# Output staging, a merged addition and interleaved token rows in a local and strided attention with an FFN

## The chip, the cores and the metric

One core of one Trainium2 chip runs the whole program. The metric is the device time of one execution in microseconds (us); times are medians over runs. TensorE multiplies matrices and writes PSUM; VectorE (DVE), ScalarE (ACT) and GpSimd (POOL) do elementwise work; SyncE (SP) issues all the DMA transfers. Each engine works through its own queue in a fixed order, and an instruction that waits holds up all that is behind it.

## The reference

Inputs q, k, v have the shape (8 batch entries, 8 heads, 576 tokens, 64). Heads 0 to 3 see a local window, heads 4 to 7 every 32nd token. The attention's output, 4608 tokens by 512, goes through a two-layer network with GELU between.

```python
pos = np.arange(S)
rel = pos[:, None] - pos[None, :]
mask_local = (rel >= 0) & (rel < 32)
mask_strided = (rel >= 0) & (pos[None, :] % 32 == pos[:, None] % 32)
scores = np.where(masks, scale * (q @ k.T), -1e9)
x = (softmax(scores) @ v).transpose(0, 2, 1, 3).reshape(4608, 512)
h = x @ w_in                      # 512 x 2048
g = 0.5 * h * (1 + erf(h / sqrt(2)))
out = g @ w_out                   # 2048 x 512
```

## The kernel before, in words

**Tiles.** The 4608 tokens are cut into rows of 32, 16 rows (512 tokens) make a tile, and there are nine tiles, t = 0 to 8. `order_of_rows` (line 110) says which rows: after the first two tiles, all of a batch entry's rows 4 to 17 follow one another, and the last tile holds rows 16 and 17 of entry 6 and rows 4 to 17 of entry 7. The hidden 2048 columns are 16 slices f of 128. Every operand of a matmul is split into a high and a low part, and a product is the sum of three matmuls (high by high, low by high, high by low).

**Plain tiles (0 to 2, `ffn`).** For each f: the product with w_in into a PSUM bank H0 or H1 (line 991), GELU and a copy of the high part on ACT (L1017, L1018), the low part on DVE (L1020), and four output blocks a = 0 to 3 of 128 tokens, accumulated over f in the banks O0 to O3 (`second`, L1041).

**Crossed tiles (3 to 8, `crossed`, `pair`).** The first product is made in the manner of Strassen and Winograd: two slices f = 2p and 2p + 1 form a cycle p, with seven block products instead of eight, each of six matmuls of 256 columns (`product`, L1190). The weights of a block product are loaded from HBM into one of 22 pieces of memory in turn (L1179); two of these lie in the buffer `xll`. Half of the token columns are even rows, half are odd rows, so in these tiles the rows of the output stand in the order 0, 2, 4, ..., 14, 1, 3, ..., 15 of the tile. A cycle has two banks; the products 1, 6 and 7 accumulate in one half of the second, and copies of it (L1218, ACT or DVE) and of product 5 go to the memory `extra`. DVE additions (`plus`, L1224) put them together: `c11` after product 2, `c12` after product 3, both 256 columns in the two halves of the first bank, and `c22` after product 7, which product 4 then accumulates on. GELU (L1250), the copy of the high part (L1251) and the low part (L1253) follow for each of the two banks. The GELU results rotate through three pairs of buffers (`third`).

**Order.** TensorE's order is written by hand: a string of products and output blocks of the cycle before, `"1oo256o37oo4ooo"`, where o is one output block (the first four are those of slice 2p, the next those of 2p + 1). All other engines' orders come from a planner (`Plan.run`): a list scheduler with a cost and a due time for each operation. From 140 us of planned time on (`steady`) it holds back work on ACT and DVE that would delay operations marked urgent, such as these copies, additions and GELUs. It counts 0.05 us from the end of an operation to its user (0.2 for TensorE) and 0.6 us on SP for the storing of a block.

**Storing (`leave`).** After the last f, each output block is copied from its bank by ACT or DVE (L1069) into a staging buffer and stored (L1088). From tile 2 on there are two staging buffers in `xlh`: blocks 0 and 2 share one, 1 and 3 the other, and the copy waits for the store before. In crossed tiles a block's four rows of 32 tokens aren't neighbours in the output, so it leaves in four transfers of 64 KB. In the last tile block 3 is made in two halves of 256 columns: its last two slices accumulate in two spare banks, and DVE adds them to what was copied early to another buffer (L1067, L1280).

**Strided heads.** Their attention is done without TensorE: POOL multiplies (L885, L902), DVE sums up (L890, L907), with batch entries' data loaded at L869. The local heads use TensorE (L589, L634) and DVE and ACT for the softmax (L652, L659).

## Time and profile before

| what | value |
|---|---|
| median of 3 runs | 845.63 us (845.23 to 846.0) |
| the profiled execution | 843.62 us |
| its span, first to last instruction | 841.8 us |
| mean granted clock of TensorE | 0.997 |
| TensorE busy | 810.8 us, 96% |
| DVE, ACT, POOL busy | 576.5, 475.7, 522.7 us |
| DMA moved | 172.62 MB |

The span is what the trace covers; 1.82 us of the execution lie outside it. A busy engine isn't a bound by itself; the chain of waits tells which work the end of the program hung on, and the timeline of an engine shows in brackets how long it sat idle before an instruction and what ended that.

### The profile page before, as it was taken

The numbers are of one execution on the slowest core, as the hardware profiler recorded it, in microseconds if no ns is written. First come the engines' busy times: TensorE is split into PE (matmuls) and PEld (weight loads), VectorE is DVE, ScalarE is ACT, GpSimd is POOL, SyncE is SP. The second block draws the span as 40 slices with busy tenths as digits, with TensorE's granted clock in tenths as the row PEclk, the third lists the DMA queues.
The fourth block names the chain that finished last, engine by engine and source line by source line (L and its number), as shares of the span: only waits on it lengthen the run. The fifth ranks groups of instructions, "written<-read, shape, count | busy, mean of one in ns | idle before, by whom it ended". The sixth has DMA issues, their size and how long they took to land.

```text
span 841.8 us, 18074 instructions
## 1 busy us (share of the span) xinstructions
PE 810.8 (96%) x6702; PEld 707.7 (84%) x6702; DVE 576.5 (68%) x1248; ACT 475.7 (57%) x1006; POOL 522.7 (62%) x448
## 2 busy tenths in 40 slices
PE   2899999999999999999999999999999999999996
PEld 2788888888888888989898989898889889898995
DVE  6887866866666778677877786577876787353332
ACT  6799955753584368546654676455745573232221
POOL 5736678799878877895777677646985576000000
PEclk9999999999999999999999999999999999999998
DMA  9947467323635677667876776768677576466401
GB/s 351 425 190 288 139 183 255 124 71 124 194 132 165 226 230 249 223 216 236 254 228 208 236 263 182 260 209 245 218 248 252 179 250 199 146 194 207 151 1 50
DMA packets 85430, 172.62 MB, mean 205 GB/s; under 512 B 10336, under 2 KB 24928, under 8 KB 83040
## 3 DMA queue, kind: packets, MB, share of 16 engines
q1 hardware_dynamic: 85344, 171.48, 61.1%
q8 instruction: 53, 0.87, 0.4%
q14 instruction: 33, 0.27, 0.1%
HBM read 143.13 MB, written 24.12 MB: 199 GB/s over the span
## 4 chain that ended last, share of the span: by engine, by line
PE 91%; DVE 2%; ACT 2%; DMA 2%; issue 1%; SPq 1%; POOL 0%; DVEq 0%; ACTq 0%; POOLq 0%
PE banks L1041 45%; PE banks L1190 27%; PE banks L991 15%; PE banks L634 2%; PE banks L589 1%; DMA sv<-in_vs_dram 1%; DMA out_dram<-xlh_ob 1%; DMA lq_qk<-in_qk_dram 1%; PE banks L608 1%; SPq L1088 0%; DVE xsl L777 0%; DVE banks L1224 0%; SPq L1179 0%; ACT w_pt L659 0%; DVE pt L652 0%
## 5 line engine op out<-in xcount | busy, mean ns | idle before, releaser
L1190 PE MATMUL banks<-w_wt,w_wt 128*128 128x256 f32 x1308 | 186.5, 284 | 2.3 <-DVE gl_all L1253 1.7
L1190 PEld LDWEIGHTS banks<-w_wt,w_wt 128*128 128x128 f32 x1308 | 173.6, 191 | 10.2 <-DVE gl_all L1253 1.9
L1041 PE MATMUL banks<-w_wt,gh_all 128*128 128x512 f32 (+1 forms) x514 | 160.6, 394 | 0.0
L1250 ACT ACTIVATE banks<-banks 128x512 f32<-128x512 f32 x96 | 55.9, 582 | 130.8 <-DVE banks L1224 95.3
L1041 PE MATMUL banks<-w_wt,gh 128*128 128x512 f32 x384 | 118.4, 389 | 0.0
L1224 DVE TENSOR_TENSOR banks<-banks,w_extra 128x256 f32<-128x256 f32 x144 | 61.2, 428 | 80.5 <-PE banks L1190 71.4
L1041 PE MATMUL banks<-w_wt,gl_all 128*128 128x512 f32 (+1 forms) x257 | 99.8, 388 | 0.0
L1041 PEld LDWEIGHTS banks<-w_wt,gh_all 128*128 128x128 f32 x514 | 88.5, 190 | 11.3
L1041 PE MATMUL banks<-w_wt,w_wt 128*128 128x512 f32 x360 | 95.4, 393 | 0.0
L1041 PEld LDWEIGHTS banks<-w_wt,gh 128*128 128x128 f32 x384 | 71.7, 188 | 14.5
L1041 PE MATMUL banks<-w_wt,gl 128*128 128x512 f32 x192 | 74.8, 390 | 1.0 <-DVE gl L1020 1.0
L1041 PEld LDWEIGHTS banks<-w_wt,w_wt 128*128 128x128 f32 x360 | 63.7, 189 | 10.1
L1218 ACT COPY w_extra<-banks 128x256 f32<-128x256 f32 x69 | 24.3, 374 | 84.0 <-DVE banks L1224 42.6
L1190 PEld LDWEIGHTS banks<-xsh,w_wt 128*128 128x128 f32 x352 | 53.3, 188 | 12.4 <-ACT w_extra L1218 3.5
L1020 DVE TENSOR_TENSOR gl<-banks,gh 128x512 fp32r<-128x512 f32 (+1 forms) x50 | 33.4, 667 | 41.9 <-ACT gh L1018 41.8
L1253 DVE TENSOR_TENSOR gl_all<-banks,gh_all 128x512 fp32r<-128x512 f32 x64 | 44.0, 687 | 25.2 <-ACT gh_all L1251 24.5
L1017 ACT ACTIVATE banks<-banks 128x512 f32<-128x512 f32 (+1 forms) x50 | 28.4, 567 | 56.7 <-PE banks L991 56.5
L1190 PE MATMUL banks<-xsh,w_wt 128*128 128x256 f32 x352 | 56.7, 283 | 2.7 <-ACT w_extra L1218 1.9
L1041 PEld LDWEIGHTS banks<-w_wt,gl_all 128*128 128x128 f32 x257 | 48.3, 188 | 10.8
L991 PE MATMUL banks<-xsh,w_wt 128*128 128x512 f32 (+1 forms) x200 | 54.2, 389 | 0.0
L991 PE MATMUL banks<-xlh,w_wt 128*128 128x512 f32 (+1 forms) x200 | 53.2, 384 | 0.0
L1218 DVE COPY w_extra<-banks 128x256 f32<-128x256 f32 x75 | 30.5, 420 | 19.3 <-PE banks L1190 18.2
(893 smaller groups left out, 1809.0 us busy)
## 6 DMA issues: line engine op xcount, KB each, us to landing
w_wt<-block SPq DMA_DIRECT2D x306, 256.0 KB, 3.1
w_raw<-in_w_dram SPq DMA_DIRECT2D x16, 1023.8 KB, 12.4
lq_qk<-in_qk_dram SPq DMA_DIRECT2D x8, 1280.0 KB, 5.8
lq_v<-in_vl_dram SPq DMA_DIRECT2D x8, 1024.0 KB, 5.4
block<-w_extra SPq DMA_DIRECT2D x32, 256.0 KB, 2.6
xll_all<-block SPq DMA_DIRECT2D x30, 256.0 KB, 2.9
block<-w_wt SPq DMA_DIRECT2D x24, 256.0 KB, 3.5
out_dram<-xlh_ob SPq DMA_DIRECT2D x92, 64.0 KB, 2.2
```

Of the source, the lines that this page charges most:

```text
L589: nc.tensor.matmul(sb[j][i]()[quarter(g), c + r * 64:c + (r + 1) * 64], qv[half(i), r, a, b * QB:(b + 1) * QB], kv[half(i), r, a, b * QB:( ...
L608: nc.tensor.matmul(x, vv[quarter(g), c, h, :], pv[quarter(g), c, h, :], start=(c == 0), stop=(c == g % 2), tile_position=(g * QB, i * 64))
L634: nc.tensor.matmul(xb[b]()[half(i), c:c + QB], vv[half(b), a, 2 * r + i, :], bv[half(b), a, 2 * r + i, :], start=True, stop=True, tile_pos ...
L991: nc.tensor.matmul(hp()[:, 0:c1 - c0], w1[f][:, lw, c, :], rx, start=((c, part) == (2, 0)), stop=((c, part) == end))
L1017: A.activation(hp()[:, 0:N], hp()[:, 0:N], AF.Gelu)
L1020: o3 = plan.add({"DVE": dve(N)}, lambda e, hp=hp, a_=a_, b_=b_, N=N: V.tensor_tensor(b_()[:, 0:N], hp()[:, 0:N], a_()[:, 0:N].bitcast(F32) ...
L1041: nc.tensor.matmul(acc()[:, 0:d1 - d0], x().bitcast(F32R)[:, c:c + P], w2[f][:, y, d0:d1], start=start and i == 0, stop=stop and i == 2)
L1190: nc.tensor.matmul(acc(), w[:, a, c, :], x[b][:, c, :], start=first and n == 0, stop=n == 5, skip_group_check=not first)
L1218: o = plan.add({"ACT": act(256), "DVE": dve(256)}, lambda e: (V.tensor_copy if e == "DVE" else A.copy)(dst(), src()), deps + old, 0, src.b ...
L1224: o = plan.add({"DVE": dve(256)}, lambda e: V.tensor_tensor(dst(), a(), b(), ALU.add), deps, 0, a.banks + dst.banks + [extra], name=name)
L1250: A.activation(hb(), hb(), AF.Gelu)
L1253: d = plan.add({"DVE": dve(TT)}, lambda e, hb=hb, gh=gh, gl=gl: V.tensor_tensor(gl().bitcast(F32R), hb(), gh().bitcast(F32), ALU.subtract) ...
```

## The change

Staging: `xll` becomes staging too, so that from tile 2 on each of the four blocks has a buffer of its own (blocks 0 and 1 in `xlh`, 2 and 3 in `xll`); the ring of weight pieces goes from 22 to 20. Addition: `c11` and `c12` become one DVE addition of 512 columns after product 3. Last tile: the copy of the high part and the low part of the GELU are written with the 32 tokens of a block's four rows interleaved (token m of row c at place 4m + c of the block), so that a block whose rows lie evenly in one batch entry leaves in one transfer; its blocks are finished in the order 0, 2, 1, 3, with blocks 0 and 1 copied by ACT and 2 and 3 by DVE. TensorE's order in the first crossed cycle becomes `"1o256o37o4o"` (it has four output blocks to place). The three GELU buffer pairs are used in another order. The planner counts 0.5 us after a POOL operation and 5% more for its duration, from 140 us on.

```diff
+ORDERS = "1o256o37o4o", "1oo256o37oo4ooo"
+    POOL_LAT = 0.5
...
-            at[op] = max([d.end + (self.PE_LAT if d.engine == "PE" else self.LAT) for d in op.deps] + [op.rel])
+            at[op] = max([d.end + (self.PE_LAT if d.engine == "PE" else self.POOL_LAT if d.engine == "POOL" and d.end > self.steady
+                                   else self.LAT) for d in op.deps] + [op.rel])
...
-                dur = op.eng[e]
+                dur = op.eng[e] * (1.05 if e == "POOL" and now > self.steady else 1.0)
...
-        for a in range(NJ):
-            k = a % 2, t < PLAIN - 1
+        for a in (0, 2, 1, 3) if last else range(NJ):
+            k = (a if t >= PLAIN - 1 else a % 2), t < PLAIN - 1
...
-                ob, first = Area(staged[0], a % 2 * DM, DM), free.get(NF - 1)
+                ob, first = Area(staged[a // 2], a % 2 * DM, DM), free.get(NF - 1)
...
-                    "DVE" if a % 2 else "ACT": 0.7 / n}
+                    "DVE" if a > 1 else "ACT": 0.7 / n}
...
+                    by = 1 if t < PLAIN else 2
                     runs = []
                     for i, (b, r) in enumerate(rows):
-                        if runs and rows[i - 1] == (b, r - 1):
+                        if runs and rows[i - 1] == (b, r - by):
...
+                    if last and len(runs) == 1:
+                        to = out[runs[0][2]:runs[0][2] + QB, cols]
+                        to = bass.AP(tensor=to.tensor, offset=to.offset, ap=[
+                            [DM, QB], [by * QB * DM, 4], [1, cols.stop - cols.start]])
+                        nc.sync.dma_start(to, ob()[:, cols])
+                        return
                     for c0, c1, d in runs:
-                        nc.sync.dma_start(out[d:d + (c1 - c0) * QB, cols], ob()[c0 * QB:c1 * QB, cols])
+                        if by == 1:
+                            nc.sync.dma_start(out[d:d + (c1 - c0) * QB, cols], ob()[c0 * QB:c1 * QB, cols])
+                            continue
+                        for c in range(c0, c1):
+                            e = d + (c - c0) * by * QB
+                            nc.sync.dma_start(out[e:e + QB, cols], ob()[c:P:4, cols] if last else ob()[c * QB:(c + 1) * QB, cols])
...
-        staged.append(buf("xlh", [P, N2, TT], "ob", 1, F32, mats))
-        xl = buf("xll", [P, N2, TT], "all", 1, F32R, mats)
+        staged.extend([buf("xlh", [P, N2, TT], "ob", 1, F32, mats), buf("xll", [P, N2, TT], "ob", 1, F32, mats)])
...
-        pieces.extend([(Area(xl, x * DM, DM), [h_last[NF - 1]], xl) for x in range(2)])
+        third.append([Area(held[NF - 1], 2 * DM * x, DM) for x in range(2)])
         third.extend([buf(x, [P, TT], f"all{i}", 2, F32R, mats) for x in ("gh", "gl")] for i in range(2))
-        third.append([Area(held[NF - 1], 2 * DM * x, DM) for x in range(2)])
...
+    def by_rows(x, t):
+        return x().rearrange("p (a c m) -> p a c m", a=NJ, m=QB) if t == NT - 1 else x()
+
+    def turned_rows(x, t):
+        return x().rearrange("p (a m c) -> p a c m", a=NJ, m=QB) if t == NT - 1 else x()
...
-        c11 = plus(r1, r1, s1, [P_[2], k1], f"c{t}.{p}.11")
...
-        c12 = plus(r3, r3, s2, [P_[3], k2], f"c{t}.{p}.12")
+        c1 = plan.add({"DVE": dve(512)}, lambda e: V.tensor_tensor(bi(), bi(), Area(extra, 1024, 512)(), ALU.add),
+                      [P_[2], P_[3], k1, k2], 0, [bi, extra], name=f"c{t}.{p}.1")
+        c1.urgent = URGENT[1]
...
-                A.copy(gh().bitcast(F32R), hb())
+                A.copy(turned_rows(gh, t).bitcast(F32R), by_rows(hb, t))
...
-                gl().bitcast(F32R), hb(), gh().bitcast(F32), ALU.subtract), [g], 0, [hb] + hold, name=f"gl{t}.{f}")
+                turned_rows(gl, t).bitcast(F32R), by_rows(hb, t), turned_rows(gh, t).bitcast(F32), ALU.subtract), [g], 0, [hb] + hold, name=f"gl{t}.{f}")
...
-        for x in "1oo256o37oo4ooo":
+        for x in ORDERS[c is not cycles[0]]:
...
-    for x, y in zip(*cycles[-1]["o"]):
-        plan.pe += [x, y]
+    x, y = cycles[-1]["o"]
+    for a in (0, 2, 1, 3, 4):
+        plan.pe += [x[a], y[a]]
```

## Rows read from the trace of the kernel before

**Rows 1.** The page's chain of waits, shares of the span by engine.
```profile
PE 91%; DVE 2%; ACT 2%; DMA 2%; issue 1%; SPq 1%; POOL 0%; DVEq 0%; ACTq 0%; POOLq 0%
```
**Rows 2.** Busy time by stretches: stretch, length, then PE, PEld, DVE, ACT, POOL, clock, DMA.
```profile
40.00:298.00 258.00, 258.00 (x1856) 213.29 (x1855) 183.98 (x350) 166.13 (x315) 196.66 (x161) 1.00 0.51 176
363.30:826.40 463.10, 460.28 (x3917) 412.70 (x3917) 310.55 (x690) 234.04 (x517) 247.59 (x204) 1.00 0.64 206
```
**Rows 3.** Timeline of PE: start, duration, line, operation; in brackets idle before, releaser.
```profile
307.95 0.98 PE L1190 MATMUL banks<-w_wt,w_wt 128*128 128x256 f32 x6 [1.73 <-DVE gl_all L1253]
...
360.30 0.97 PE L1190 MATMUL banks<-w_wt,w_wt 128*128 128x256 f32 x6 [0.48 <-DVE banks L1224]
...
402.42 0.73 PE L1190 MATMUL banks<-xsh,w_wt 128*128 128x256 f32 x4 [0.31 <-DVE w_extra L1218]
...
446.68 0.74 PE L1190 MATMUL banks<-xsh,w_wt 128*128 128x256 f32 x4 [0.19 <-ACT w_extra L1218]
...
492.00 0.74 PE L1190 MATMUL banks<-xsh,w_wt 128*128 128x256 f32 x4 [0.67 <-ACT w_extra L1218]
...
593.68 0.73 PE L1190 MATMUL banks<-xsh,w_wt 128*128 128x256 f32 x4 [1.06 <-ACT w_extra L1218]
...
759.34 0.74 PE L1190 MATMUL banks<-xsh,w_wt 128*128 128x256 f32 x4 [0.52 <-DVE w_extra L1218]
```
**Rows 4.** Timeline of the end, from 828 us on.
```profile
830.49 3.62 SPq L1088 DMA_DIRECT2D out_dram<-xlh_ob  x8
...
834.03 0.42 DVE L1067 TENSOR_TENSOR lead_all<-banks,lead_all 128x256 f32<-128x256 f32 x1 [0.22 <-PE banks L1041]
834.21 1.77 SPq L1088 DMA_DIRECT2D out_dram<-lead_all  x4
...
837.95 1.77 SPq L1088 DMA_DIRECT2D out_dram<-lead_all  x4
```
**Rows 5.** Timeline of SP at the end of tile 2: stores of whole blocks.
```profile
300.23 1.03 SPq L1088 DMA_DIRECT2D out_dram<-xlh_ob  x2
```
**Rows 6.** DMA issues: count, KB each, median us from issue to landing.
```profile
out_dram<-xlh_ob SPq DMA_DIRECT2D x3, 256.0 KB, 2.6
...
out_dram<-lead_all SPq DMA_DIRECT2D x8, 32.0 KB, 1.6
```
**Rows 7.** Timeline, block copies that waited for a store.
```profile
491.08 0.58 ACT L1069 COPY xlh_ob<-banks 128x512 f32<-128x512 f32 x1 [1.91 <-DMA out_dram<-xlh_ob]
...
757.80 0.69 DVE L1069 COPY xlh_ob<-banks 128x512 f32<-128x512 f32 x1 [2.75 <-DMA out_dram<-xlh_ob]
```
**Rows 8.** Groups by line and shape: busy us, mean ns; idle before, releasers.
```profile
L1224 DVE TENSOR_TENSOR banks<-banks,w_extra 128x256 f32<-128x256 f32 x144 | 61.2, 428 | 80.5 <-PE banks L1190 71.4 <-issue 6.1 <-ACT pt L659 2.2
...
L1253 DVE TENSOR_TENSOR gl_all<-banks,gh_all 128x512 fp32r<-128x512 f32 x64 | 44.0, 687 | 25.2 <-ACT gh_all L1251 24.5
...
L496 ACT ACTIVATE w_raw<-lead_all 128x1024 int32<-128x1024 int16 x16 | 18.2, 1140 | 0.1
```
**Rows 9.** Timeline of a quiet cycle of the last tile, DVE and PE.
```profile
749.03 0.43 DVE L1224 TENSOR_TENSOR banks<-banks,w_extra 128x256 f32<-128x256 f32 x1 [0.90 <-PE banks L1190]
749.75 0.43 DVE L1224 TENSOR_TENSOR banks<-banks,w_extra 128x256 f32<-128x256 f32 x1 [0.29 <-PE banks L1190]
750.73 0.69 DVE L1253 TENSOR_TENSOR w_wt<-banks,w_wt 128x512 fp32r<-128x512 f32 x1 [0.55 <-ACT w_wt L1251]
...
753.71 0.88 PE L1190 MATMUL banks<-w_wt,w_wt 128*128 128x256 f32 x6
```
**Rows 10.** The chain in order of time: start, duration; one run of output blocks.
```profile
463.22 2.07 PE banks L1041 x9
```
**Rows 11.** Timeline of the first crossed cycle.
```profile
304.34 0.42 DVE L1224 TENSOR_TENSOR banks<-banks,w_extra 128x256 f32<-128x256 f32 x1
...
304.68 1.28 ACT L1250 ACT_TABLE_LOAD   x1
```
**Rows 12.** Timeline of DVE in tile 6: a sum waiting for POOL's product.
```profile
586.66 0.95 DVE L907 TENSOR_REDUCE acc_7.2_6609<-prod_v7.2.3_6588 128x64 f32<-128x768 f32 x1 [3.05 <-POOL prod_v7.2.3_6588 L902]
```

More of the change, by code (lines that the diff above doesn't have):

```diff
@@ L1242, in pair @@
         os_ = []
-        for f, hb, deps in ((i, bi, [c11, c12]), (j, bj, [P_[4], c22])):
+        for f, hb, deps in ((i, bi, [c1]), (j, bj, [P_[4], c22])):
             k = 2 * c + f - i
@@ L1266, in pair @@
             os_.append(row)
-        cycles.append({"p": P_, "o": os_, "adds": [c11, c12, c22], "t": t, "n": p})
+        cycles.append({"p": P_, "o": os_, "adds": [c1, c22], "t": t, "n": p})
     spare = [bank("S0"), bank("S1")]
```

## Prediction

> **What bounds the kernel now.** I read the chain of waits first, by engine [rows 1]: nine tenths of it is TensorE, and DVE, ACT and DMA have 2% each. So a cheaper DVE or ACT instruction is worth nothing by itself. Only three things can pay: time before TensorE starts, holes in its stream, and time after its last matmul. Next the busy time by stretches [rows 2]: from 40 to 298 us TensorE is busy for all of 258.00 us, and from 363.3 to 826.4 it lacks 463.10 - 460.28 = 2.82 us. The first 40 us stay as they are: the planner's new terms act from its 140th us on, and all other edits lie later. That leaves the holes and the end.
>
> Then the holes, from the timeline of TensorE alone [rows 3]: after 40 us there are seven, 1.73 + 0.48 + 0.31 + 0.19 + 0.67 + 1.06 + 0.52 = 4.96 us. Last the end [rows 4]: the last matmuls are taken by a DVE addition that ends at 834.03 + 0.42 = 834.45, and the span ends at 841.8. The 7.35 us between are SyncE issuing twelve more stores at 0.44 us each, and the last landing. Together 12.3 us (1.5% of the span) can be reached at all.
>
> **The end.** Before, blocks 0, 1 and 2 leave in four transfers each and block 3 in two halves of four: 20 issues, which keep SyncE occupied from 830.49 to 837.95 + 1.77 = 839.72, and the span ends 2.08 us later [rows 4]. With the new row order blocks 1 and 3 have rows of one batch entry (entry 7, rows 10, 12, 14, 16 and 11, 13, 15, 17), so block 1 takes one issue and each half of block 3 one. Blocks 0 and 2 begin with row 16 or 17 of entry 6, so they have two runs and still leave in four: 4 + 4 + 1 + 1 + 1 = 11 issues, the quick blocks last. Block 0 keeps its start, and block 2 takes the place of block 1, so the first eight end at 830.49 + 3.62 = 834.11, as now. An issue of 256 KB in one piece took 1.03 / 2 = 0.52 us [rows 5]; with 0.1 us before each (834.11 to 834.21 [rows 4]) three make 1.86 and end at 836.0. The data of block 3, ready at 834.45, no longer comes last. The landing: 32 KB took 1.6 us and 256 KB 2.6 [rows 6], the new last piece has 128 KB, so I add 0.5: 836.0 + 2.08 + 0.5 = 838.6, **3.2 us earlier**. Bounds: with issues of 0.44 and no longer landing it ends at 834.11 + 3 x 0.44 + 2.08 = 837.5 (4.3 gained); with issues of 0.88 (twice that, for a pattern of three levels) and a landing 1.0 longer, 834.11 + 2.64 + 3.08 = 839.8 (2.0 gained). I stay near the middle, by the 256 KB row, the same kind of store.
>
> **Four staging buffers.** Now two blocks share one buffer, so the copy of the third block waits until the first has landed. Idle ACT or DVE costs nothing unless an urgent copy is queued behind it, and it is: at 491.08 ACT had waited 1.91 us for a store, the copies that a product needs came next in its queue, and TensorE's hole of 0.67 follows at 492.00 [rows 3, 7]. The holes at 402.42 and 759.34 have the same cause, a DVE block copy that waits for a store ahead of the urgent work (2.75 us before the second) [rows 3, 7]. A buffer that is not shared is asked for again only a tile later, when its store has long landed. Gain 0.31 + 0.67 + 0.52 = **1.5 us** at most; at least 0, if the new order puts other waits there; I take it all, since each of the three waits has its landing named. The price is two weight pieces that lay in that memory: a ring of 20 instead of 22, at seven products per cycle still over two cycles ahead, which covers it. Stores come closer together on SyncE, with weight loads and the loads of q, k, v behind them: 16 x 0.44 = 7 us of queue at most, against more than 20 us of lead.
>
> **One addition for two.** Two DVE additions of 428 ns become one of 512 columns, priced by the nearest row of that width, 687 ns [rows 8]: 48 x (2 x 0.428 - 0.687) = 8.1 us of DVE, off the path, worth 0. But the later of the two took 0.43 after product 3; now all that is behind it comes 0.26 us later. Who waits: the GELU of the first half, its split, and product 1 of the next cycle, which overwrites that bank. In a quiet cycle the addition starts at 749.03, the split ends at 750.73 + 0.69 = 751.42, and product 1 starts at 753.71 [rows 9], so 2.29 us of cover stand against 0.26: cost 0. The next DVE addition, which product 4 waits for, starts at 749.75, just after 749.03 + 0.69 = 749.72 [rows 9], so it is not pushed either when DVE is free at that moment. Bounds: 0 and 0.26 x 48 = 12.5 us, if that moment is never free.
>
> **First cycle of the crossed tiles.** Its hole of 1.73 us at 307.95 is product 1 waiting for the split [rows 3]. There one output block moves from before product 2 to after product 4; three matmuls more, a third of the 2.07 us that nine take [rows 10], so 0.69 us, now cover that much of the wait. The merged addition does not lengthen it, because the GELU there waits for its table, loaded from 304.68 to 305.96, over a microsecond after the addition at 304.34 ended [rows 11]. Gain **0.7 us**; bounds 0 and 1.73. The staged GELU outputs change places so that the first uses memory that is free early; nothing waited for that, so 0.
>
> **The new POOL terms** (0.5 us after a POOL result, 5% on its time) move no work by themselves; they reorder the DVE, ACT and SyncE queues from 140 us on. The hole of 1.06 follows a DVE wait of 3.05 us for POOL [rows 3, 12], the kind that they should push later; but a new order makes new holes. The three holes not yet counted are 0.48 + 0.19 + 1.06 = 1.73 us: I take 0, bounds 1.73 gained and 5.0 lost (as many holes again as there are now).
>
> **Interleaved tokens** give ACT and DVE a write step of four elements in 16 GELU pairs of the last tile. The nearest row, ACT writing every second element, took 1140 ns for 1024 [rows 8], 1.11 ns each, against 0.58 us for 512 in a plain block copy [rows 7], 1.13 each: a step of two is free, and I take four as free too. Bounds: 0, and three times the copy and the subtraction, rival (c).
>
> **Sum.** 3.2 + 1.5 + 0.7 = 5.4 us: the span goes from 841.8 to 836.4 and the profiled execution from 843.62 to 838.2. The median of the runs, 845.63, lies 2.0 us above that execution; the change should take the same 5.4 from it: **840.2 us**. A measurement of this kernel can tell about 0.2%, 1.7 us, from no change.
>
> **Rivals.** (a) *The new order gives it back.* The end is gained, but DVE and ACT, reordered in every tile, open 5.0 us of new holes: 840.2 + 5.0 = 845.2, no change that can be told. For it: holes come from single queue accidents such as the 3.05 us wait [rows 12]. Against: from 40 to 298 us there is none [rows 2]. Chance 0.12.
>
> (b) *Slower: the merged addition sets the pace.* If DVE is busy with a long reduction when product 3 ends, the longer addition pushes the one for product 4, and TensorE stops by up to 0.26 us per cycle: 840.2 + 12.5 = 852.7. It decides from 5.4 / 0.26 = 21 of the 48 cycles on. Against it: the quiet cycle, where both fit [rows 9], and how little TensorE lacks now [rows 2]; for it: they fit to 0.03 us. Chance 0.06.
>
> (c) *The interleaved writes are slow.* If the copy (0.58, as in [rows 7]) and the subtraction (0.69) each took three times as long, 2.54 us would go into the 2.29 us of cover [rows 9]: 0.25 in each of eight cycles, and at most 2.54 more behind the last pair: 840.2 + 2.0 + 2.5 = 844.7. Doubled (1.27 us), they would hide but for the end. No row shows a step of four, so chance 0.05. The Trainium skill, "SBUF — State Buffer", section "Door 1: The DMA port swizzle", speaks for this rival: consecutive accesses within one 16-byte line run at full rate, each crossing to a new line pays, and four fp32 are the limit of what is free; this change writes at that limit.
>
> (d) *The single transfer is no quicker.* A destination of three levels might issue or land slowly; the lower bound of the end, 2.0 gained, gives 840.2 + 1.2 = 841.4. Chance 0.05.
>
> **How the numbers follow.** The forecast has 0.72. Faster by over 0.2% (under 843.9): the forecast and (d), 0.77; within 0.2%: (a) and (c), 0.17; slower: (b), 0.06. The range starts near all best bounds together, 4.3 + 1.5 + 1.73 + 1.73 = 9.3, less what seldom comes together: 837.0. Above, it takes in the forecast with an end of 2.0, no other gain and up to half a microsecond of new holes, 844.2, and leaves out (a), (b) and (c) only in their full size.
>
> **What would show it.** Right: eleven stores at the end and the span ending about 4 us after the last DVE addition; no block copy of the crossed tiles behind a store; a hole near 308 us of about 1 us; 48 additions of 512 columns near 0.69 us. Wrong: holes of TensorE summing to 5 us or more after 140 us, product 4 waiting for DVE in many cycles, or GELU copies of the last tile well over 0.58 us.

## The result and the profile after

| | before | after |
|---|---|---|
| median of the runs | 845.43 us (4 runs, 844.2 to 846.0) | **835.4 us** (4 runs, 835.27 to 835.59) |
| profiled execution, its span | 843.62, 841.8 us | 835.29, 833.5 us |

The ratio is 0.9883 (95% interval 0.9866 to 0.9901): faster by 1.2%, with an interval clear of 1. That is 10.0 us where 5.4 were forecast, and 1.6 us below the range. The span is 8.3 us shorter.

**The three views of [rows 1 to 3] after.** The page's busy times and chain, then the windows (columns as in [rows 2]), then the only hole of more than 0.12 us in TensorE's timeline after 40 us:

```profile
PE 809.7 (97%) x6702; PEld 709.0 (85%) x6702; DVE 595.5 (71%) x1225; ACT 478.5 (57%) x1001; POOL 510.0 (61%) x431
...
PE 92%; DMA 4%; POOL 2%; DVE 1%; SPq 0%; issue 0%; POOLq 0%
```
```profile
40.00:298.00 258.00, 258.00 (x1857) 213.37 (x1856) 190.84 (x360) 166.29 (x316) 186.74 (x148) 1.00 0.51 174
298.00:362.00 64.00, 64.00 (x628) 57.26 (x630) 48.91 (x122) 40.92 (x98) 48.48 (x45) 1.00 0.74 240
362.00:820.00 458.00, 457.68 (x3817) 411.83 (x3810) 324.17 (x661) 239.19 (x514) 249.58 (x204) 1.00 0.65 209
```
```profile
399.35 0.74 PE L1203 MATMUL banks<-xsh,w_wt 128*128 128x256 f32 x4 [0.21 <-DVE w_extra L1237]
```

TensorE lacks 0.32 us from 362 to 820, where it lacked 2.82 [rows 2]. Six of the seven holes are gone. DVE and POOL are neither the gain nor the price: DVE's busy time rose by 19.0 us (576.5 to 595.5) and POOL's fell by 12.7, and they hold only 1% and 2% of the chain.

**Where the 8.3 us came from.** I compare the start of the same work in both traces, here from the chain in order of time (start, duration, work), before and after:

```profile
295.45 2.72 PE banks L1041 x12
...
826.42 7.59 PE banks L1041 x39
```
```profile
295.26 2.72 PE banks L1044 x12
...
819.56 7.61 PE banks L1044 x39
```

Output blocks at the end of tile 2 start 0.2 us earlier than before (295.45, now 295.26). The last run of output blocks starts 6.86 us earlier (826.42, now 819.56); so the crossed tiles give 6.7. From the start of the last DVE addition to the end of the span it was 841.8 - 834.03 = 7.77 us and is 833.5 - 827.20 = 6.30: the end gives 1.5.

**Holes on the two rows of TensorE.** The matmul rows showed only 4.96 us of holes [rows 3], so 6.7 us cannot have come out of them. The weight loads, which run ahead of the matmuls, show more. All waits of PEld over 0.12 us before, from 40 us on, without the standing 0.35 us at the attention's lines, and all of after:

```profile
305.24 0.77 PEld L1190 LDWEIGHTS banks<-w_wt,w_wt 128*128 128x128 f32 x6 [0.39 <-DVE banks L1224]
307.95 0.77 PEld L1190 LDWEIGHTS banks<-w_wt,w_wt 128*128 128x128 f32 x6 [1.94 <-DVE gl_all L1253]
360.30 0.77 PEld L1190 LDWEIGHTS banks<-w_wt,w_wt 128*128 128x128 f32 x6 [0.90 <-DVE banks L1224]
402.42 0.53 PEld L1190 LDWEIGHTS banks<-xsh,w_wt 128*128 128x128 f32 x4 [0.74 <-DVE w_extra L1218]
446.68 0.53 PEld L1190 LDWEIGHTS banks<-xsh,w_wt 128*128 128x128 f32 x4 [0.62 <-ACT w_extra L1218]
492.00 0.53 PEld L1190 LDWEIGHTS banks<-xsh,w_wt 128*128 128x128 f32 x4 [1.10 <-ACT w_extra L1218]
593.68 0.53 PEld L1190 LDWEIGHTS banks<-xsh,w_wt 128*128 128x128 f32 x4 [1.49 <-ACT w_extra L1218]
594.73 0.77 PEld L1190 LDWEIGHTS banks<-w_wt,w_wt 128*128 128x128 f32 x6 [0.28 <-DVE w_extra L1218]
604.72 0.53 PEld L1190 LDWEIGHTS banks<-xsh,w_wt 128*128 128x128 f32 x4 [0.33 <-DVE w_extra L1218]
670.40 0.53 PEld L1190 LDWEIGHTS banks<-xsh,w_wt 128*128 128x128 f32 x4 [0.25 <-ACT w_extra L1218]
759.34 0.53 PEld L1190 LDWEIGHTS banks<-xsh,w_wt 128*128 128x128 f32 x4 [0.95 <-DVE w_extra L1218]
```
```profile
304.19 0.77 PEld L1203 LDWEIGHTS banks<-w_wt,w_wt 128*128 128x128 f32 x6 [0.26 <-DVE banks L1243]
305.77 0.76 PEld L1203 LDWEIGHTS banks<-w_wt,w_wt 128*128 128x128 f32 x6 [0.33 <-DVE w_wt L1273]
307.85 0.54 PEld L1203 LDWEIGHTS banks<-xsh,w_wt 128*128 128x128 f32 x4 [0.16 <-DVE gl_all L1273]
399.35 0.53 PEld L1203 LDWEIGHTS banks<-xsh,w_wt 128*128 128x128 f32 x4 [0.65 <-DVE w_extra L1237]
534.52 0.77 PEld L1203 LDWEIGHTS banks<-w_wt,w_wt 128*128 128x128 f32 x6 [0.54 <-DVE banks L1243]
```

The sums are 8.99 and 1.94 us; the difference of 7.05 answers to the 6.7 us that the work moved, where the matmul rows' 4.96 - 0.21 = 4.75 falls 1.9 short. The Trainium skill, "Perfetto Trace Analysis", section "Tensor Engine Instruction (MATMUL, LD_WEIGHTS)", says that the profiler estimates the end of a TensorE instruction and doesn't observe it; these two sums agree with that.

**The end, and the first cycle.** The end of the timeline after (against [rows 4]); then the first crossed cycle (against [rows 11]) on PE, DVE and ACT:

```profile
823.65 2.44 SPq L1103 DMA_DIRECT2D out_dram<-xlh_ob  x4
...
826.19 2.45 SPq L1103 DMA_DIRECT2D out_dram<-xll_ob  x4
...
827.20 0.42 DVE L1070 TENSOR_TENSOR lead_all<-banks,lead_all 128x256 f32<-128x256 f32 x1 [0.22 <-PE banks L1044]
828.74 0.58 SPq L1095 DMA_DIRECT2D out_dram<-xlh_ob  x1
829.41 1.23 SPq L1095 DMA_DIRECT2D out_dram<-lead_all  x2
```
```profile
303.06 0.70 DVE L1256 TENSOR_TENSOR banks<-banks,w_extra 128x512 f32<-128x512 f32 x1 [0.78 <-PE banks L1203]
...
303.79 0.58 ACT L1270 ACTIVATE banks<-banks 128x512 f32<-128x512 f32 x1 [0.93 <-DVE banks L1256]
...
306.60 1.28 ACT L833 ACT_TABLE_LOAD   x1
```

Eleven stores, as forecast, but those from interleaved rows (every fourth partition) take 2.44 / 4 = 0.61 us to issue, not 0.44. In the first cycle the GELU now starts 0.03 us after the addition; the exponential whose table had to be swapped back before it [rows 11] runs after the GELUs.

### The profile page after: what moved, and what is told of

The parts are those of the page before. It is cut to its first block, busy times and chain, and to the rows that moved or that the text cites. A ratio compares the mean times of both kernels' runs of the same rounds, so it can differ in the third digit from the quotient of the medians.

```text
span 833.5 us, 17940 instructions
## 1 busy us (share of the span) xinstructions
PE 809.7 (97%) x6702; PEld 709.0 (85%) x6702; DVE 595.5 (71%) x1225; ACT 478.5 (57%) x1001; POOL 510.0 (61%) x431
## 4 chain that ended last, share of the span: by engine, by line
PE 92%; DMA 4%; POOL 2%; DVE 1%; SPq 0%; issue 0%; POOLq 0%
PE banks L1044 46%; PE banks L1203 28%; PE banks L994 15%; PE banks L637 2%; DMA w_k<-in_k_dram 2%; PE banks L592 1%; DMA w_raw<-in_w_dram 1%; DMA sk<-in_ks_dram 1%; POOL prod_oqo1.1.1_541 L941 0%; DVE xsl L780 0%; POOL w_wt L515 0%; POOL prod_oqo1.0.1_485 L941 0%; SPq L1338 0%; DMA out_dram<-xlh_ob 0%; POOL prod_oqo1.0.0_505 L941 0%; DVE acc_6.4_5988 L910 0%
## 5 line engine op out<-in xcount | busy, mean ns | idle before, releaser
L1203 PE MATMUL banks<-w_wt,w_wt 128*128 128x256 f32 x1440 | 204.7, 284 | 0.1
L1203 PEld LDWEIGHTS banks<-w_wt,w_wt 128*128 128x128 f32 x1440 | 191.1, 191 | 8.5 <-DVE banks L1243 0.8
L1237 DVE COPY w_extra<-banks 128x256 f32<-128x256 f32 x84 | 35.5, 422 | 53.5 <-PE banks L1203 52.7
L1044 PEld LDWEIGHTS banks<-w_wt,w_wt 128*128 128x128 f32 x360 | 63.7, 189 | 10.1
L1273 DVE TENSOR_TENSOR gl_all<-banks,gh_all 128x512 fp32r<-128x512 f32 x64 | 48.3, 755 | 30.6 <-ACT gh_all L1271 30.4
L1203 PEld LDWEIGHTS banks<-xsh,w_wt 128*128 128x128 f32 x384 | 58.6, 188 | 8.8 <-DVE w_extra L1237 0.6
L1203 PE MATMUL banks<-xsh,w_wt 128*128 128x256 f32 x384 | 61.2, 282 | 0.2 <-DVE w_extra L1237 0.2
L1237 ACT COPY w_extra<-banks 128x256 f32<-128x256 f32 x60 | 22.2, 371 | 64.0 <-PE banks L1203 63.8
L1256 DVE TENSOR_TENSOR banks<-banks,w_extra 128x512 f32<-128x512 f32 x48 | 33.5, 697 | 30.8 <-PE banks L1203 30.5
```

Of the source, the lines that this page charges most:

```text
L1044: nc.tensor.matmul(acc()[:, 0:d1 - d0], x().bitcast(F32R)[:, c:c + P], w2[f][:, y, d0:d1], start=start and i == 0, stop=stop and i == 2)
L1203: nc.tensor.matmul(acc(), w[:, a, c, :], x[b][:, c, :], start=first and n == 0, stop=n == 5, skip_group_check=not first)
L1237: o = plan.add({"ACT": act(256), "DVE": dve(256)}, lambda e: (V.tensor_copy if e == "DVE" else A.copy)(dst(), src()), deps + old, 0, src.b ...
L1256: c1 = plan.add({"DVE": dve(512)}, lambda e: V.tensor_tensor(bi(), bi(), Area(extra, 1024, 512)(), ALU.add), [P_[2], P_[3], k1, k2], 0, [b ...
L1273: d = plan.add({"DVE": dve(TT)}, lambda e, hb=hb, gh=gh, gl=gl: V.tensor_tensor(turned_rows(gl, t).bitcast(F32R), by_rows(hb, t), turned_r ...
```

## The experiments

Ratios are to the kernel before, run beside each kernel on the same chip; its medians there were 845.35 to 845.78. "Taken out" means the changed kernel less one part, "alone" the kernel before plus that part.

**1. One part taken out at a time.** The planner's terms for POOL taken out:

```diff
-    POOL_LAT = 0.5
+    POOL_LAT = 0.05
-                dur = op.eng[e] * (1.05 if e == "POOL" and now > self.steady else 1.0)
+                dur = op.eng[e] * 1.0
```


> The changed kernel (835.4 us) with the planner's two POOL terms taken out, everything else kept. Theory A, each edit removes its own holes: the three holes of the kernel before that stood behind late POOL results (near 360, 447 and 594 us, together 3.9 us on the timeline of weight loads) come back, about 839.3 us. Theory B, the gain belongs to no single edit, a new order of the queues simply fell well: the time may land anywhere from 834 to 842 and the holes stand in new places. Theory C, the four buffers and the first cycle's string carry all of it: no change, 835.4 us within 0.5.

Measured 836.28 us, 0.9892 (0.9877 to 0.9906): 0.9 us lost. ACT's timeline shows where most of it goes: the table for GELU is loaded again in the first cycle, and a hole of 0.79 us follows at 307.12 (smaller ones, 0.36 and 0.21 us, stand at 525.10 and 634.34).

```profile
303.34 1.28 ACT L1270 ACT_TABLE_LOAD   x1
304.63 0.58 ACT L1270 ACTIVATE banks<-banks 128x512 f32<-128x512 f32 x1
```

Staging shared again (two buffers for four blocks):

```diff
-            k = (a if t >= PLAIN - 1 else a % 2), t < PLAIN - 1
+            k = a % 2, t < PLAIN - 1
-                ob, first = Area(staged[a // 2], a % 2 * DM, DM), free.get(NF - 1)
+                ob, first = Area(staged[0], a % 2 * DM, DM), free.get(NF - 1)
```


> The changed kernel with two staging buffers that the blocks share, as before; the ring stays at 20 pieces. Theory A: the waits of block copies for stores come back at five tile ends, with three holes of together 2.8 us on the timeline of weight loads, and at the end block 1 waits for the store of block 2 or 0, up to 1 us: 838.2 to 839.2 us. Theory B: anywhere from 834 to 842. Theory that the POOL terms carry all of it: holes stay away although copies wait, 835.4 to 836.4 us.

Measured 843.06, 0.9967 (0.9949 to 0.9986): 7.7 us lost, the largest loss by far and more than any of the three theories had. A block copy waits for a store, the output block that needs its bank waits for the copy, TensorE stops, and the granted clock falls to 0.86 in the stretch behind (timelines of ACT and PE, and the window 668 to 680; 1.00 in the changed kernel):

```profile
670.25 0.58 ACT L1072 COPY xlh_ob<-banks 128x512 f32<-128x512 f32 x1 [2.78 <-DMA out_dram<-xlh_ob]
...
670.89 0.91 PE L1044 MATMUL banks<-w_wt,gh_all 128*128 128x512 f32 x2 [2.53 <-ACT xlh_ob L1072]
```
```profile
668.00:680.00 12.00, 9.47 (x163) 7.80 (x163) 6.06 (x30) 3.56 (x7) 4.34 (x3) 0.86 0.63 190
```

Between the value products on either side this stretch costs 4.3 us, and a hole of 1.23 us at 489.93 another 1.5. The end is about 1 us longer too: blocks 0 and 2, which share a buffer, now follow one another, and block 2's copy waits for block 0's stores.

Two additions again (`c11`, `c12` instead of `c1`):

```diff
+        c11 = plus(r1, r1, s1, [P_[2], k1], f"c{t}.{p}.11")
...
-        c1 = plan.add({"DVE": dve(512)}, lambda e: V.tensor_tensor(bi(), bi(), Area(extra, 1024, 512)(), ALU.add),
-                      [P_[2], P_[3], k1, k2], 0, [bi, extra], name=f"c{t}.{p}.1")
-        c1.urgent = URGENT[1]
+        c12 = plus(r3, r3, s2, [P_[3], k2], f"c{t}.{p}.12")
...
```


> The changed kernel with the two DVE additions of 256 columns in place of the one of 512. Theory A: DVE has 8 us more to do, none of it on the path: 835.4 us within 0.5, the additions again 0.43 us each. Theory B: DVE's queue is reordered in all 48 cycles, so the time may move by 1 to 4 us either way.

Measured 837.72, 0.9906 (0.9891 to 0.9921): 2.3 us lost by the medians, with holes of 0.59 (400.85) and 0.18 us (460.17). The profiled execution (836.56 us, the fastest of the four) lost only 0.9 us of span, which holes of this size can account for; where the other three lost the rest, no trace shows.

No interleaving (rows of the last tile plain, 64 KB transfers, order 0, 2, 1, 3 kept):

```diff
-                    if last and len(runs) == 1:
+                    if False:
...
-        return x().rearrange("p (a c m) -> p a c m", a=NJ, m=QB) if t == NT - 1 else x()
+        return x()
```


> The changed kernel without the interleaved tokens: the last tile's GELU copies write in plain order, and each block of the last tile leaves in four transfers of 32 partitions side by side; the order of the blocks (0, 2, 1, 3) and the four buffers stay. Expected: the copies fall from 1.07 to 0.59 us and the subtractions from 1.10 to 0.69 us without any gain, as they are covered; issues cost 0.44 us each again instead of 0.61, but there are 20 of them: they end 20 x 0.45 = 9.0 us after 823.65, at 832.7, and the span about 2.1 later, 834.8 instead of 833.5, so 836.7 us. If the step of four partitions is not what makes an issue cost 0.61 us, the issues keep 0.61 and the span ends near 838, 840 us.

Measured 836.78, 0.9896 (0.988 to 0.9913): 1.4 us lost. SP's timeline at the end shows 0.44 us per issue again, but twenty of them:

```profile
824.35 1.73 SPq L1103 DMA_DIRECT2D out_dram<-xlh_ob  x4
...
829.95 3.63 SPq L1103 DMA_DIRECT2D out_dram<-lead_all  x8
```

The old string in the first cycle:

```diff
-ORDERS = "1o256o37o4o", "1oo256o37oo4ooo"
+ORDERS = "1oo256o37oo4ooo", "1oo256o37oo4ooo"
```


> The changed kernel with the old string for TensorE's order in the first crossed cycle (two output blocks before product 2). In the changed kernel GELU of the first bank follows the addition at once (303.79 us), with no table load between, and its split ends about when product 1 of the next cycle starts (305.77). Theory A, half of the old hole went with the table load and half with the moved block: with one block less in front, product 1 is ready 0.7 us before the split: a hole of about 0.7 us near 305.5, 836.1 us. Theory B, the string alone took away the hole: 1.7 to 1.9 us come back, 837.2 us. Theory C, the string does nothing: 835.4.

Measured 837.85, 0.9905 (0.9888 to 0.9922): 2.4 us lost. The hole at 307.28 is back with 1.14 us, but the planner's order changed further on too (holes of 0.79, 1.40 and 0.47 us at 401.47, 591.66 and 715.11), so the 2.4 us aren't the string's alone.

The five losses add up to 7.7 + 0.9 + 2.3 + 1.4 + 2.4 = 14.7 us, more than the 10.0 that all parts bring: they overlap. Every edit that the planner sees can give all queues a new order.

**2. Parts alone, and in steps.** The edits are those of the change, applied to the kernel before.

> The kernel before with the two POOL terms of the planner alone. Theory A: the holes behind late POOL results (near 360, 447 and 594 us, 3.9 us on the timeline of weight loads) go or shrink, those behind stores stay: 841.5 to 843 us. Theory that shared staging is what makes the other holes too, since a queue held up by a store is late for everything after it: nothing gained, 844.5 to 846 us.

> The kernel before with four staging buffers alone (ring of 20 pieces, old order at the end, old additions, old string, no POOL terms). By the run that gave the changed kernel shared buffers back (7.7 us slower), staging is the largest part: some 2.8 us of holes behind stores, the end (block 2 no longer waits for block 0's landing, so its four issues no longer stand last), and the spread between executions. Theory A: 845.4 - 2.8 - 1 = 841.5 us, with runs closer together. Theory B, buffers pay only with the POOL terms and the new order: 844 to 846 us.

> The kernel before with the first crossed cycle's string and the order of the three GELU buffer pairs alone. In the first trace of the kernel before, the hole of 1.73 us near 308 us passed at a granted clock of 1.00; in the second trace, and in that of the kernel with four buffers alone, the clock fell to 0.72 over the 6 us around it, and product 1 to the next output blocks took 1.5 us more. Theory A, the hole costs its own length and, in most executions, a stretch at the lower clock: with one more block in front the hole shrinks by 0.7 to about 1 us, and if the clock then stays up, 845.6 - 0.7 - 1.5 = 843.4 us, with a granted clock of 1.00 from 306 to 312 us. Theory B, the clock's fall has nothing to do with the hole: only 0.7 us are gained, 844.9 us, and the clock falls there as often as before.

The POOL terms alone: 847.18, 1.0019 (1.0005 to 1.0033), a little slower, with holes of 1.43 and 1.47 us at 404.09 and 494.01 where there were 0.31 and 0.67. Four buffers alone: 844.31, 0.9983 (0.9974 to 0.9993), 1.4 us gained. The three holes behind a store (402.42, 492.00 and 759.34 before) are gone from its trace; the other four stay (the largest still 1.73 at 308.09, and 0.71 at 594.56 instead of 1.06), and new ones of 1.04 and 0.55 us stand at 588.63 and 596.08. The first cycle's string alone (with the order of the GELU buffers): 844.78, 0.9988 (0.9976 to 1.0), 0.9 us gained at the edge of what can be told from no change; its hole shrank to 0.84 us with a granted clock of 1.00 behind it, and new ones of 1.48, 1.10 and 1.83 us came at 358.52, 581.78 and 629.77. No part alone is worth what it is worth in the whole. So I built the change up, first buffers and first cycle, then the merged addition as well.

> The kernel before with four staging buffers and the first crossed cycle's edits (string and order of the GELU buffers), nothing else: two additions, old end, no POOL terms. Alone these two gave 1.4 and 0.9 us. If gains add up: 845.6 - 2.3 = 843.3 us. If each part alone is held back by holes that the other parts remove (the order is only free of holes when no queue is ever held up), together they give more than their sum: 838 to 841 us.

> The same and the one addition of 512 columns; the end and the POOL terms are still those of before. The changed kernel lacked 2.3 us when the two additions were given back, 1.4 when the end was, 0.9 without the POOL terms, so what is left here should be about 835.5 + 1.4 + 0.9 + (block order and engines of the end, up to 1) = 838 to 839 us. If the addition is worth nothing without the POOL terms: the same as the kernel without it, within 0.5.

841.72 (0.9953, 0.9939 to 0.9967) and 838.21 (0.9912, 0.9898 to 0.9927): here the addition brought 3.5 us. The timelines of DVE near 625 us, without and with the merged addition, show a large piece of it:

```profile
626.69 0.69 DVE L893 TENSOR_REDUCE sc_8.1_7109<-prod_q8.1.3_7130 128x8 f32<-128x512 f32 x1 [2.66 <-POOL prod_q8.1.3_7130 L888]
627.30 0.42 DVE L1243 TENSOR_TENSOR banks<-banks,w_extra 128x256 f32<-128x256 f32 x1
```
```profile
621.82 0.70 DVE L1256 TENSOR_TENSOR banks<-banks,w_extra 128x512 f32<-128x512 f32 x1 [0.31 <-PE banks L1203]
622.54 0.43 DVE L1243 TENSOR_TENSOR banks<-banks,w_extra 128x256 f32<-128x256 f32 x1
625.19 0.69 DVE L893 TENSOR_REDUCE sc_8.1_7105<-prod_q8.1.3_7117 128x8 f32<-128x512 f32 x1 [2.22 <-POOL prod_q8.1.3_7117 L888]
```

DVE waits over 2 us for POOL in both. Without the merged addition `c22` stands behind that wait, and TensorE has a hole of 2.16 us at 627.77; with it `c22` stands ahead, and there is none. The steps, by the medians: before 845.6, four buffers 844.3, first cycle 841.7, one addition 838.2, the end 836.3 (the changed kernel without its POOL terms, in part 1), POOL terms 835.4.

**3. What a hole costs besides its length.** The changed kernel's gain by the medians (10.0) is larger than by the profiled executions (8.3). The kernel before once more, profiled again:

> The kernel before, once more, for a second trace of the same instructions. If the holes are accidents of timing within one order (a transfer that lands late), other holes or other lengths stand in this trace, while the order of every queue is the same; the span may differ from 841.8 us by up to 2 us, and the holes by the same. If they are fixed by the order, the same seven holes stand there with the same lengths within 0.1 us.

846.84 us, span 845.0, with the same order in all queues. The seven holes stand in the same places, one of them 0.32 us longer and another 0.23, and an eighth of 0.21 us stands at 651.85: so in these two traces the order mostly fixes where the holes stand, and not how long each is. The window from 306 to 312 us of this execution, behind the hole of 1.73 us, and that of the execution of [rows 3]:

```profile
306.00:312.00 6.00, 4.27 (x18) 3.49 (x17) 5.11 (x8) 4.83 (x9) 5.30 (x4) 0.72 0.75 219
```
```profile
306.00:312.00 6.00, 4.27 (x30) 3.80 (x30) 4.92 (x9) 5.21 (x8) 5.67 (x4) 1.00 0.79 252
```

Busy for 4.27 us in both, TensorE did 18 matmuls in the one and 30 in the other: the granted clock fell behind the hole to 0.72 of 2.4 GHz on average, from 310 to 312 us to 0.50, its lower level of 1.2. From product 1 to the same later product it took 7.31 us (308.29 to 315.60) against 5.78: 1.53 us more. Of the 3.2 us that this span is longer, another 0.35 lie before the crossed tiles and about 1.3 in the longer holes. To test the clock's part in a place where nothing was wrong, the changed kernel got seven more copies of a bank onto itself on ACT ahead of one GELU of tile 5 (they compute nothing; a first version with the same purpose issued none of them and measured 835.51, the changed kernel once more):

```diff
             def gelu(e, hb=hb, gh=gh, f=f):
+                for _ in range(7 if (t, f) == (5, 8) else 0):
+                    A.copy(hb(), hb())
```


> The changed kernel with one hole made on purpose: in tile 5, cycle 4, ACT copies the first bank onto itself seven times (about 4 us) ahead of GELU, without the planner's knowledge, so every queue keeps its order. (In the run before with this aim the copies were not emitted: the condition read the last value of a loop; that run stands as a second measurement of the changed kernel, 835.51 us.) Cover is about 2.0 us, so TensorE should stand still for 1.5 to 2.5 us near 516. Theory A, a hole of this length can cost the clock too: 838.5 to 840 us in some executions, with a granted clock under 1 in the 6 us after it. Theory B, a hole costs its own length: 837 to 838 us with a clock of 1.00.

Measured 839.31, 0.9925 (0.9909 to 0.9942): 3.9 us lost, the span 3.8 longer (837.3). Timeline of PE, and the window behind the hole:

```profile
528.55 1.59 PE L1203 MATMUL banks<-w_wt,w_wt 128*128 128x256 f32 x6 [2.08 <-DVE gl_all L1275]
529.94 1.05 PE L1044 MATMUL banks<-w_wt,gh_all 128*128 128x512 f32 x2
```
```profile
528.00:531.00 3.00, 2.45 (x9) 2.26 (x10) 2.60 (x6) 1.52 (x4) 1.97 (x1) 0.61 0.00 0
```

Product 1 started at 526.49 in the changed kernel, so the hole itself costs 2.1 us. From there to the tile's value products it is 541.25 - 528.55 = 12.70 us against 537.50 - 526.49 = 11.01: 1.7 more, at a granted clock of 0.61. So this hole of 2.08 us costs 3.8, not 2.1: here the clock's share is shown. But not every such hole has it. From 40 us on, all kept traces together hold eight holes of 1.73 us or more on the matmul rows. Behind four the granted clock fell to 0.50: this one, the 1.73 of the second trace of before and of the kernel with four buffers alone, and the 2.53 of the one with shared staging. Behind the other four it stayed at 1.00: 1.73 in the first trace of before and with the POOL terms alone, 1.83 at 629.77 and 2.16 at 627.77 (part 2). It stayed there behind all twenty of 0.67 to 1.48 us, too. What decides it, no run here shows.

**4. The end, further.** The last tile's blocks 1 and 3 stored from ACT's queue instead of SP's:

```diff
-                        nc.sync.dma_start(to, ob()[:, cols])
+                        (A if a % 2 else nc.sync).dma_start(to, ob()[:, cols])
...
-                ops.append(plan.add({"SP": 0.6}, store, [o], at_step((t + 1) * NF), kept, kb=256 / n,
+                ops.append(plan.add({"ACT" if last and a % 2 else "SP": 0.6}, store, [o], at_step((t + 1) * NF), kept, kb=256 / n,
```


> The changed kernel with the last tile's stores of blocks 1 and 3 issued by ACT instead of SP. In the changed kernel SP issues 11 stores without a break from 823.65 to 830.64, and the span ends 2.86 us later. If the row of issues on one queue sets the end: SP is done with blocks 0 and 2 at 828.64, ACT with its three at about 828.3, and the span ends 2.0 us earlier: 833.4 us. If the transfers themselves or their landing set it, the end moves by less than 0.5 us: 835 us.

Measured **833.99**, 0.986 (0.9845 to 0.9876): the best version, 1.4 us below the changed kernel. The two queues issue side by side (timeline of the end), and from the start of the last DVE addition to the end of the span it is 832.3 - 828.13 = 4.17 us, 2.1 less than in the changed kernel, near the 2.0 expected. A hole of 0.81 us at 400.34 instead of 0.21 took part of the gain.

```profile
827.12 2.46 SPq L1103 DMA_DIRECT2D out_dram<-xll_ob  x4
827.31 0.65 ACTq L1095 DMA_DIRECT2D out_dram<-xlh_ob  x1
828.06 1.22 ACTq L1095 DMA_DIRECT2D out_dram<-lead_all  x2
...
828.13 0.42 DVE L1070 TENSOR_TENSOR lead_all<-banks,lead_all 128x256 f32<-128x256 f32 x1 [0.22 <-PE banks L1044]
```

Can a block leave in one transfer without interleaved tokens? The row (3 or 4 of them) becomes the outermost level of the transfer, seven issues in all:

```diff
...
+                            if c1 - c0 > 1:
+                                to = bass.AP(tensor=to.tensor, offset=to.offset, ap=[
+                                    [by * QB * DM, c1 - c0], [DM, QB], [1, cols.stop - cols.start]])
...
```


> The changed kernel without the interleaved tokens, but with each run of rows still leaving in one transfer, whose outermost level is then the row (four or three of them) and not the token (32): 2 + 2 + 1 + 1 + 1 = 7 issues. If the order of levels does not matter to a transfer: the issues end at about 828.3 instead of 830.64, and the span 2.3 us earlier, 833.1 us. If a transfer whose outermost level is 4 lands slowly, each of 192 to 256 KB takes several us more than the 2.1 to 2.4 us seen now, and the time is 836 us or more.

Measured 842.03, 0.9954 (0.9938 to 0.997): 6.6 us slower than the changed kernel. The last issue ends at 830.58, and the span 9.7 us later, with the DMA engines at a share of 0.20 (SP's timeline; window of the wait). The seven stores, five of them with 3 or 4 as their outermost level, share this wait: 75 GB/s over 9 us are 675 KB, and the last has only 128:

```profile
827.76 2.82 SPq L1097 DMA_DIRECT2D out_dram<-lead_all  x2
```
```profile
831.00:840.00 9.00, 0.00 (x0) 0.00 (x0) 0.00 (x0) 0.00 (x0) 0.00 (x0) 0.55 0.20 75
```

The Trainium skill, "DMA: Bandwidth & Descriptors", section "Rules for kernel authors", says that an outermost dimension of less than 16 confines a transfer to so many of the 16 engines; the share of 0.20 (0.25 and 0.27 in the two stretches of 3 us to 837) agrees with 4 of 16 (0.25). In the changed kernel the outermost level is the 32 tokens, and the last landing is 2.9 us. The same with ACT's queue,

> Both together: row-outermost transfers, and blocks 1 and 3 issued by ACT. If the order of levels does not matter, the last data (ready at 827.6) is issued at once and the span ends about 2.9 us later: 830.6 us of span, 832.4 us. If row-outermost transfers land slowly, the time is near that of the kernel with them on SP alone, less at most 1 us.

gave 843.26, 0.9967 (0.9953 to 0.9981), 1.2 us slower still: a second queue doesn't help such transfers here.

## Why the prediction was right or wrong

**What bounds the kernel: right in kind, the holes mis-sized.** Only holes and the end paid; DVE's extra 19 us cost nothing. The step that failed is the sum of the holes, "4.96 us". It was read on matmul rows; on the weight loads they are 8.99 us, and the 12.3 us within reach should have been over 16. The crossed tiles gave 6.7 us, where 2.2 were forecast, more than all the holes that the forecast knew of. With the end that makes the 8.3 of the traces instead of 5.4. Taken from the median, 8.3 would give 837.3 us, just inside the range; the last 1.7 come from a second step, on the median, at the end of this section.

**The end: right mechanism, mis-sized (3.2 forecast, 1.5 measured).** The step that failed here is "the first eight end at 834.11, as now". They are read from every fourth partition now and take 0.61 us each instead of 0.44: 826.19 + 2.45 - 823.65 = 4.99 us instead of 3.62, 1.37 lost. The last landing took 2.86 us (833.5 - 830.64) instead of 2.58, 0.28 lost. 3.2 - 1.65 leaves about 1.5. The single issues (0.58 and 0.61) were near the 0.52 taken.

**Four staging buffers: right mechanism, mis-sized (1.5 forecast).** On the weight loads the three holes are 0.74 + 1.10 + 0.95 = 2.8 us, and with four buffers alone they are gone, as forecast. In the changed kernel no copy of a crossed tile waits for a store of `xlh` or `xll`; before, eight did, for 15.5 us together. The 7.7 us of the taken-out run aren't this term alone: they hold a hole of 2.53 us that the kernel before doesn't have, the clock behind it, and a longer end.

**First cycle: direction right, mis-sized (0.7 forecast, 1.6 by the weight loads).** With the string alone the hole shrank from 1.73 to 0.84, a little more than the 0.69 forecast. The rest of it went because the table is no longer loaded ahead of the GELU: the step "the GELU there waits for its table" took for fixed what the planner's order decides. Of the kernels with the new string, the four without the POOL terms (0.79 to 0.84 us of hole) load GELU's table at about 303 to 304 us; the changed kernel and all the others with these terms don't, and have no hole there on the matmul rows. So the POOL terms have a share in this gain.

**One addition: "worth 0" was wrong.** As work it is worth nothing: 48 additions at a mean of 697 ns (687 forecast), and product 4 never waits for more than 0.54 us. But it changes what stands ahead of what in DVE's queue. The edit brought 3.5 us in the steps and 2.3 in the taken-out run; of these the hole of 2.16 us at 627.77 is traced to such an order, the rest is not. Rival (b), 12.5 us lost, didn't happen.

**POOL terms: 0 was near.** 1.5 us slower alone, 0.9 us faster in the whole, within the bounds of 1.73 and -5.0. What decides it isn't shown; whether the reordering meets a free queue is a guess, and I know no way to read it from the trace of before.

**Interleaving as a write pattern: "free" was wrong, "covered" right.** The last of the 16 GELU pairs on ACT and DVE, timeline after:

```profile
820.21 1.07 ACT L1271 CAST gh_all<-banks 128x512 fp32r<-128x512 f32 x1
...
821.31 1.08 DVE L1273 TENSOR_TENSOR gl_all<-banks,gh_all 128x512 fp32r<-128x512 f32 x1 [1.01 <-ACT gh_all L1271]
```

Against 0.59 and 0.69 us at a step of one that is 0.48 + 0.39 = 0.9 us more, inside the 2.29 us of cover [rows 9]: the last tile has no hole. So rival (c) had the mechanism and not the size; the prediction had named copies well over 0.58 us as a sign of being wrong, and they came without costing anything. With plain rows the subtraction takes 0.69 us again. The rule of the Trainium skill cited there ("SBUF — State Buffer", "Door 1: The DMA port swizzle") is that an access which crosses to a new 16-byte line pays. The trace agrees: a step of four fp32 takes 1.8 times as long on ACT and 1.6 times on DVE, which also reads `gh` at that step. A step of four, which the prediction took for the limit of what is free, was not free.

**"The same 5.4 from the median": wrong.** The profiled execution of before (843.62 us) is faster than all the other 71 executions of that kernel on record (843.86 us and more), while that of the changed kernel lies near its median. So the gain by the medians is 1.7 us larger than by the traces. Part of it can be the clock behind the hole at 308, which cost 1.5 of the 3.2 us lost in the second trace; in the changed kernel's trace it stays at 1.00 there. How much of the 1.7 it is in a median execution stays open.

Rivals (a) and (d) didn't happen; something like (a) is what the POOL terms or the first cycle do alone. Of the other signs, the span ends 5.9 us after the last DVE addition and not "about 4". Booked by place on the weight loads, the staging holes gave 1.3 us more than forecast, the first cycle (0.39 + 1.94 - 0.26 - 0.33 - 0.16 = 1.6) 0.9 more, and the other holes (3.87 before, 1.19 after) 2.7 that were forecast as 0; the end gave 1.7 less; and 1.7 is the choice of the profiled execution. That accounts for the miss, but not for which edit removed which of the other holes. No edit but the POOL terms was aimed at them, these alone made holes longer, and that so many went with the new order is, as far as these runs show, luck.

## What to carry to other kernels

Read the holes of a dense matmul stream on the weight loads, compare the starts of the same work before and after, and allow for a loss of clock behind a hole of two microseconds: it came behind four of eight here, and where it was measured it cost nearly as much again. Where a planner sets the queues, an edit's worth lies less in the instructions it saves than in which waiting instruction ends up ahead of urgent work, so parts must be measured in the whole and not alone. A store on the path at the end did best here with a large outermost level (32 against 4) and two issuing queues.

## What the hardware showed that was not expected

- Behind a single hole of 1.73 or 2.08 us in a dense stream the granted clock fell to between 0.61 and 0.72 over the next microseconds, which cost 1.5 and 1.7 us; behind others of 1.73, 1.83 and 2.16 us it stayed at 1.00.
- A transfer whose source takes every fourth partition took 0.61 us to issue, a contiguous one of the same 64 KB 0.44.
- The last of seven stores, five of them with 3 or 4 as their outermost level, ended 9.7 us after its issue, at a DMA share of 0.20; the last of eleven with 32 outermost, of the same bytes, 2.9 us after its own.
